# Second expert layer of a fused attention and mixture-of-experts kernel: fp32 second products become three fp32r products of halves, and first weights are loaded straight into two alternating places

## The chip, the cores and the metric

The kernel runs as one program on one core of a Trainium2 chip. The metric is the device time of one launch in microseconds (us); lower is better. Five engines run side by side, each with its own instruction stream in program order: PE (TensorE, matrix products; its weight loads are listed as PEld), DVE (VectorE), ACT (ScalarE), POOL (GpSimd, which also issues the indirect transfers) and SP (SyncE, which issues the plain transfers).

## The reference, cut to what matters

Attention over 4 batches, 12 heads, 448 positions, then two layers of experts over the 1,792 resulting rows. Only the second layer is touched:

```
N, D, E, F = (1792, 768, 8, 1024)
cap = N // E
...
# greedy assignment: best (token, expert) logit first, at most cap tokens an expert
...
for e in range(E):
    mask = assigned == e
    h = np.maximum(x[mask] @ w1[e], 0.0)
    out[mask] = h @ w2[e]
```

Each expert gets exactly 224 tokens. All data is fp32.

## The kernel before, in words

The second layer is `moe2`. It handles the eight experts in the order in which the assignment fills them. Per expert there are 48 *first products* (line L2063: 8 blocks f of 128 hidden columns, 6 slices k of 128 inputs; 224 tokens move against a 128x128 block of w1), a relu per block f (L2067, ACT), and 32 *second products* (L2077: two halves h of 112 tokens, two column halves of 384, 8 slices k). All operands are fp32. Four *turns* (L2051) transpose the tokens that were fetched for the next expert.

While the experts run, an `Assigner` works out which expert comes next and which tokens it has. A first round of it runs ahead of the experts, six more and a short last step run while they do. Such a round goes through all engines: `bids` (L1588 to L1611, with transposes L1598 on PE and copies L1600 on ACT), `count` (a column of comparisons each in L1678, L1680, L1682 on DVE, products L1643 on PE, transposes L1717), `settle` (L1721 to L1782, product L1752) and `put` (L1814 to L1838, products L1831). Its products stand in the same PE stream as the expert products, and PE takes its stream in order.

The place of each assigner step in the streams is fixed when the program is written, by `Pace`: a model with one clock per engine. Every piece of expert work calls `work(engine, cost, ready)`, which first writes out those assigner steps that the model would start earlier. The costs are constants in us, such as 0.19 for a first and 0.325 for a second product.

Weights come by `pump` (SP queue) in slices of 128 rows into six raw places, first the 6 slices of w1, then the 8 of w2; `split` copies each slice into `w1t` or `w2t`, odd slices on POOL (L2031), even ones on ACT (L2034). Products read the copies. The fourth w1 slice of an expert (`LATE`) waits for the fetch of its tokens, by a one-element POOL write (L2017) behind the two gathers (L2043).

Of the kernel before, what the change touches and what calls it, by code (L numbers as in the profile page):

```python
# [1933 lines left out]
def moe2(tc, consts, wt, qkv, x0, asn, w1, w2, y, out):  # L1934
# [8 lines left out]
    with ExitStack() as ctx:  # L1943
        ctx.enter_context(tc.manual_schedule())
        p2 = ctx.enter_context(tc.tile_pool(name="m2p", bufs=1, reuse_waits="tile"))
        ps = ctx.enter_context(tc.tile_pool(name="m2ps", bufs=1, space=PSUM))
        w1t, w2t = wt
        bank = [ps.tile([128, 512], F32, name=f"bank{i}") for i in range(8)]
        pg2, po3, px0 = bank[2:4], bank[4:7], bank[7]
        turns = cycle(bank[:2])  # L1950
        asn.bank, asn.counts = lambda: next(turns), lambda: next(turns)

        raws = [t[:, FF * i : FF * i + FF] for t in qkv for i in range(3)]
        xt = p2.tile([128, KD, CAP], F32, name="xtt")
        ht = p2.tile([128, KF, CAP], F32, name="ht")
        zr = x0[0]
        xgs = [p2.tile([CP, YW], F32, name=f"xg{i}") for i in range(2)]

# [3 lines left out]
        def first_product(f):  # L1962

            return (po3 + pg2)[f // 2][:, CAP * (f % 2) : CAP * (f % 2) + CAP]
# [30 lines left out]
        clock, work = pace.clock, pace.work  # L1995


        nload, nsplit = 0, 0

        arrival, there, done = {}, {}, {}  # L2000
        fetched = []
# [5 lines left out]
        def pump(eng=nc.sync, most=6):  # L2007
            nonlocal nload
            while nload < nsplit + most:
                n, first, k = piece(nload)  # L2010
                if n >= len(regs):
                    break
                if (n, first, k) == (n, True, LATE) and n:

                    if (n, 1) not in fetched:
                        break
                    nc.gpsimd.memset(raws[nload % 6][0:1, 0:1], 0.0)  # L2017
                r, w, wd = raws[nload % 6], w1 if first else w2, FF if first else DM
                clock["d"] = max(clock["d"], clock["p"] + DELAY, choice[n]) + wd * 1.43e-3
                arrival[nload] = clock["d"]  # L2020
                eng.dma_start(out=r[:, :wd], in_=w[bass.ds(regs[n], 1), 128 * k : 128 * (k + 1), :].rearrange("a p f -> p (a f)"))
                nload += 1

        def split(n, first, k):
            nonlocal nsplit
            assert piece(nsplit) == (n, first, k) and nload > nsplit
            r = raws[nsplit % 6]
# [8 lines left out]
            if nsplit > 1:  # L2036
                pump()

        def gather(n, h):
            clock["d"] = max(clock["d"], work("g", 1.03) + GATHER) + 0.97  # L2040
# [16 lines left out]
        def acc(n, pg, f, k, shared=False):  # L2057
            fs = slice(128 * f, 128 * f + 128)
            check = dict(skip_group_check=shared)

            t = max(there[n, True, k], there["x", 0, k // 3], there["x", 1, k // 3])
            done[f] = work("p", 0.19, t)
            nc.tensor.matmul(pg, lhsT=w1t[:, k, fs], rhs=xt[:, k, :], start=k == 0 and not (shared and f % 2), stop=k == KD - 1, **check)  # L2063
# [26 lines left out]

        for h in range(2):
            gather(0, h)
        for r in raws[FIRST:6]:
            nc.gpsimd.memset(r[0:1, 0:1], 0.0)
        few = nc.values_load(asn.regs[0:1, E : E + 1], engines=tuple(ALL), min_val=0, max_val=1)
        start = nload, nsplit, known, list(regs), dict(asn.__dict__)

        def experts(compact):
            nonlocal nload, nsplit, known
            nload, nsplit, known = start[:3]  # L2100
            regs[:] = start[3]
            choice[:] = [0.0]
            fetched.clear()
            asn.__dict__.update(start[4])
            arrival.update((i, 0.0) for i in range(FIRST))
            pace.start(phases(compact), g=2.0, d=3.5)
            ready.update({0: 4.5, 1: 5.5})
            split(0, True, 0)
# [5 lines left out]
            for g in turns:  # L2114
                for _ in g:
                    pass
            split(0, True, 1)
            for n in range(E):
                turns, gathered, turned = [], 0, 0
                splits = iter(range(KD) if n + 1 < E else ())  # L2120

                def ahead(t):

                    nonlocal gathered, turned
                    if n + 1 == E:
                        return
                    if known > n + 1 and gathered < 2:
                        gather(n + 1, gathered)
                        gathered += 1
                    elif t >= 17:  # L2130
                        if turned < 4 and gathered > turned // 2 and ready[turned // 2] <= clock["p"]:
                            if len(turns) == turned:
# [6 lines left out]
                        if t % 2 and nload > nsplit and arrival[nsplit] <= clock["p"] + EARLY:  # L2139
                            k = next(splits, None)  # L2140
                            if k is not None:
                                split(n + 1, True, k)

                for t in range(32):
                    k2 = t // 2 + 2
                    if n and t % 2 == 0 and 2 <= t <= 16:
                        relu(product(t // 2 - 1), t // 2 - 1)
                    if n == 0 and 7 <= t < 7 + KF:
                        split(0, False, t - 7)
                    if t % 2 == 0:  # L2150
                        if n == 0 and k2 < KD:
                            split(0, True, k2)
                        elif n and k2 < KF:
                            split(n, False, k2)
                    if n and t == 3:
                        store(n - 1, 1)
                    if t == 25:
                        store(n, 0)
                    ahead(t)
                    pump()  # L2160
                    if t < 16:
                        if n:
                            f, a = divmod(t, 2)
                            for k in range(3 * a, 3 * a + 3):
                                acc(n, product(f), f, k)
                        elif t < 6:

                            k, a = divmod(t, 2)
                            for f in range(4 * a, 4 * a + 4):
                                acc(n, first_product(f), f, k, True)  # L2170
                        elif t < 6 + KF:
                            f = t - 6
                            for k in range(3, KD):
                                acc(n, first_product(f), f, k, True)

                            for i in range(f - 1, f + 1) if f % 2 else ():
                                relu(first_product(i), i)
                    else:
# [11 lines left out]
                for k in splits:  # L2190
                    split(n + 1, True, k)
                split(n + 1, False, 0)
                split(n + 1, False, 1)
            store(E - 1, 1)

        with tc.If(few > 0):
# [7 lines left out]
SLACK = 0.3  # L2204
AHEAD = 0.5
DELAY = 3.2
EARLY = 0.3
GATHER = 1.7
FIRST = 1
LATE = 3  # L2210
# [64 lines left out]
```

## Time and profile before

| | |
|---|---|
| time, median of 3 runs | 1123.95 us (1121.79 to 1124.58) |
| the profiled execution: its time, its span | 1125.03 us, 1123.3 us |
| busy PE, DVE, ACT, POOL, share of the span | 95%, 52%, 41%, 22% |
| mean granted TensorE clock | 0.968 |

The span runs from the first to the last instruction; busy is the time in which an engine had an instruction under way. Products are pipelined: the time of one is longer than the distance to the next, and the distance is what a stream of them costs. An fp32 product appears in the trace as two records (768 records for 384 first products, 512 for 256 second ones).

### The profile page before, as it was taken

Reading aid. Unit: us, or ns where it says so; the run is one execution under the profiler, and the core shown is the slowest. Engines: PE = TensorE matmul, PEld = TensorE weight load, DVE = VectorE, ACT = ScalarE, POOL = GpSimd, SP = SyncE. Lnnn points to the kernel's source line nnn. Section 1 sums busy time; section 2 is a strip of 40 time slices with the busy share of each in tenths; the row PEclk is TensorE's granted clock in tenths of the full one; section 3 lists DMA queues with packets and bytes.
Section 4 is the critical chain, followed back from the end, with each engine's and each line's share of the span. In section 5 each row is a group of like instructions: output and inputs, shape, how many; then the busy total and the mean of one; then the engine's idle time right before and its main releaser. Section 6 shows DMA issues by size and latency. Waiting matters only on the chain. (4 is left out here: it accounts for less than half of the span.)

```text
span 1123.3 us, 16924 instructions
## 1 busy us (share of the span) xinstructions
PE 1072.6 (95%) x5360; PEld 672.4 (60%) x5360; DVE 589.6 (52%) x1565; ACT 462.9 (41%) x1043; POOL 249.4 (22%) x275
## 2 busy tenths in 40 slices
PE   8999999999998999999999998959999999999995
PEld 6555565555554555555555554548575676886782
DVE  5777877877965744455566762575546562000000
ACT  3677777677684222122422111642223232233320
POOL 4443333344201110000100201011213032033110
PEclk7899999999999999999999998958999999999998
DMA  6566566566357170627400101033665183485320
GB/s 153 124 146 148 128 153 153 117 155 141 86 165 268 44 282 31 253 106 268 163 21 29 58 29 49 11 118 136 207 216 195 66 274 133 142 274 174 131 107 27
DMA packets 81024, 153.99 MB, mean 137 GB/s; under 512 B 14270, under 2 KB 53438, under 8 KB 80768
## 3 DMA queue, kind: packets, MB, share of 16 engines
q1 hardware_dynamic: 75696, 129.20, 38.0%
q0 software_dynamic: 5200, 23.33, 6.8%
q8 instruction: 49, 0.80, 0.3%
q14 instruction: 79, 0.65, 0.2%
HBM read 113.84 MB, written 17.44 MB: 117 GB/s over the span
## 5 line engine op out<-in xcount | busy, mean ns | idle before, releaser
L962 DVE SCALAR_TENSOR_TENSOR sc<-yr,wg 128x768 bf16<-128x768 f32 x104 | 162.2, 1559 | 113.8 <-ACT yr L1127 100.3
L2077 PE MATMUL bank<-w2t,ht 128*112 128x384 f32 x512 | 176.5, 489 | 0.0
L881 PE MATMUL pg<-w1t,xt 128*128 128x512 f32 x360 | 163.2, 601 | 6.3 <-PEq L1169 5.2
L899 PE MATMUL po<-w2t,hx 128*128 128x384 f32 x480 | 163.2, 488 | 0.1
L2063 PE MATMUL bank<-xtt,w1t 128*128 128x224 f32 x768 | 156.6, 359 | 0.0
L205 DVE TENSOR_REDUCE nm<-sp 112x1 f32<-112x448 f32 x192 | 118.0, 619 | 57.9 <-PE sp L204 30.1
L2063 PEld LDWEIGHTS bank<-xtt,w1t 128*128 128x128 f32 x768 | 143.7, 192 | 4.7 <-issue 0.2
L211 ACT ACTIVATE e<-sp,nm 112x448 f32<-112x448 f32 x192 | 122.0, 636 | 52.9 <-DVE nm L205 34.2
L899 PEld LDWEIGHTS po<-w2t,hx 128*128 128x128 f32 x480 | 88.3, 190 | 58.7 <-issue 6.2
L2077 PEld LDWEIGHTS bank<-w2t,ht 128*112 128x112 f32 x512 | 86.4, 177 | 59.5 <-issue 0.7
L881 PEld LDWEIGHTS pg<-w1t,xt 128*128 128x128 f32 x360 | 67.1, 192 | 81.7 <-issue 76.9
L219 PE MATMUL tp<-ident,e 112*112 112x112 f32 x768 | 112.4, 270 | 0.4 <-DVE et L222 0.4
L232 PE MATMUL op<-et,qkv 112*64 112x448 f32 x384 | 98.9, 564 | 0.0
L219 PEld LDWEIGHTS tp<-ident,e 112*112 112x112 f32 x768 | 82.2, 135 | 26.3 <-issue 20.0
L225 ACT ACTIVATE et<-tp 112x448 f32<-112x448 f32 x144 | 78.8, 547 | 38.2 <-PE tp L219 36.7
L200 PE MATMUL sp<-bt,at 128*112 128x448 f32 x188 | 85.4, 454 | 1.0 <-DMA bt<-cut 1.0
L137 POOL TENSOR_TENSOR xn<-qkv,rr 112x512 f32<-112x512 f32 x47 | 48.1, 1055 | 109.7 <-DVE rr L128 109.7
L2067 ACT ACTIVATE ht<-bank 128x224 f32<-128x224 f32 x64 | 22.4, 357 | 107.5 <-PE bank L2063 107.3
L966 POOL DMA_INDIRECT y<-yr,ti x11 | 11.9, 1085 | 234.1 <-DVE sc L962 94.2
L200 PEld LDWEIGHTS sp<-bt,at 128*112 128x112 f32 x188 | 33.9, 180 | 47.8 <-issue 32.4
L2083 POOL DMA_INDIRECT out_dram<-x,ids x16 | 15.4, 965 | 210.6 <-ACT x L2082 210.6
L884 ACT ACTIVATE hr<-pg 128x512 f32<-128x512 f32 x30 | 17.9, 597 | 93.3 <-PE pg L881 92.0
(395 smaller groups left out, 1269.7 us busy)
## 6 DMA issues: line engine op xcount, KB each, us to landing
qkv<-in_moe_w_dram SPq DMA_DIRECT2D x104, 384.0 KB, 5.8
qkv<-in_moe_w_dram SPq DMA_DIRECT2D x48, 512.0 KB, 7.1
raw<-in_moe_w_dram SPq DMA_DIRECT2D x24, 512.0 KB, 5.8
bt<-cut SPq DMA_DIRECT2D x96, 112.0 KB, 2.3
at<-cut SPq DMA_DIRECT2D x96, 112.0 KB, 2.4
qkv<-in_v_dram SPq DMA_DIRECT2D x12, 448.0 KB, 6.6
xs<-xp SPq DMA_DIRECT2D x24, 224.0 KB, 2.9
qkv<-in_k_dram SPq DMA_DIRECT2D x11, 448.0 KB, 4.4
```

The source lines that it names most:

```text
L137: eng.tensor_tensor(out=xns[i][:, t].rearrange("p c h d -> p h c d"), in0=raws[i // 2][:, t, 2 * j : 2 * j + 2, :].rearrange("p h (c d) -> ...
L200: nc.tensor.matmul(sp, lhsT=at[:, h, cs], rhs=bt[:, h, :], start=h == 0, stop=h == 1)
L205: nc.vector.tensor_reduce(out=st["nm"][:, n : n + 1], in_=sp, axis=AX.X, op=OP.max, negate=True)
L211: nc.scalar.activation(e, st.pop(("s", n)), AF.Exp, bias=st["nm"][:, n : n + 1], accum_out=st["sm"][:, n : n + 1])
L219: nc.tensor.transpose(tp[:, kc, :], e[:, kc * CP : (kc + 1) * CP], ident[:CP, :CP])
L225: nc.scalar.activation(dst, tp, AF.Copy)
L232: nc.tensor.matmul(st["op"][h * D : (h + 1) * D, :], lhsT=raws[i // 2][:, 2, 2 * (i % 2) + h, kc * D : (kc + 1) * D], rhs=st["et"][:, h, k ...
L881: nc.tensor.matmul(pg, lhsT=xt[:, k, :], rhs=w1t[:, k, fs], start=k == 0, stop=k == KD - 1)
L899: nc.tensor.matmul(po[n], lhsT=hx[:, k, :], rhs=w2t[:, kk, cs], start=kk == 0, stop=kk == KF - 1)
L962: nc.vector.scalar_tensor_tensor(sc, yr[:, 0:DM], 1.0, wge[:, :, e], op0=OP.mult, op1=OP.mult, accum_out=yr[:, DM + e : DM + e + 1])
L2063: nc.tensor.matmul(pg, lhsT=w1t[:, k, fs], rhs=xt[:, k, :], start=k == 0 and not (shared and f % 2), stop=k == KD - 1, **check)
L2077: nc.tensor.matmul(po, lhsT=ht[:, k, ts], rhs=w2t[:, k, cs], start=k == 0, stop=k == KF - 1)
```

## The change

First products stay fp32, but w1 is loaded straight to where PE reads it, in two places that alternate by expert (`w1s[n % 2]`: `w1t`, and the memory of `w2t` seen as six slices). A slice of w1 for expert n may be loaded when n is at most `firsts + 1`; `firsts` is raised when the last first product of an expert has been written. w2 gets eight raw places. Each slice of it is split into a high half `w2h` (fp32r, by ACT) and a low half `w2l`, the difference (fp32r, by POOL). The relu gives `hh` (fp32r, ACT) and `hl`, the difference (fp32r, DVE, which reads the products' bank again). A second product is then hh*w2h + hh*w2l + hl*w2h, three fp32r products of the same size into the same bank. The model's costs become 0.38 for a first and 0.53 for a second product.

```diff
-        w1t, w2t = wt
+        w1s = wt[0], wt[1].rearrange("p k f -> p (k f)").rearrange("p (k f) -> p k f", f=FF)
+        w2h = p2.tile([128, KF, DM], F32R, name="w2h")
+        w2l = p2.tile([128, KF, DM], F32R, name="w2l")
...
-        raws = [t[:, FF * i : FF * i + FF] for t in qkv for i in range(3)]
+        raws = [qkv[i // 4][:, DM * (i % 4) : DM * (i % 4) + DM] for i in range(KF)]
...
-            while nload < nsplit + most:
+            while most is None or nload < most:
                 n, first, k = piece(nload)
-                if n >= len(regs):
+                if n >= len(regs) or (n > firsts + 1 if first else KF * n + k >= nsplit + KF):
                     break
+                r = w1s[n % 2][:, k, :] if first else raws[k]
...
-            h, wd = (w1t, FF) if first else (w2t, DM)
-            if k % 2:
-                there[n, first, k] = work("g", 0.1 + wd * 1.1e-3, arrival[nsplit])
-                nc.gpsimd.tensor_copy(out=h[:, k, :], in_=r[:, :wd])
-            else:
-                there[n, first, k] = work("s", 0.1 + wd * 8.3e-4, arrival[nsplit])
-                nc.scalar.activation(h[:, k, :], r[:, :wd], AF.Copy)
+            t = work("s", 0.1 + DM * 8.3e-4, arrival[n, False, k])
+            nc.scalar.activation(w2h[:, k, :], r, AF.Copy)
+            there[n, False, k] = work("g", DM * 2.5e-3, t)
+            nc.gpsimd.tensor_tensor(out=w2l[:, k, :], in0=r, in1=w2h[:, k, :].bitcast(F32), op=OP.subtract)
...
-            done[f] = work("p", 0.19, t)
-            nc.tensor.matmul(pg, lhsT=w1t[:, k, fs], rhs=xt[:, k, :], ...)
+            done[f] = work("p", 0.38, t)
+            nc.tensor.matmul(pg, lhsT=w1s[n % 2][:, k, fs], rhs=xt[:, k, :], ...)
...
-            there["h", f] = work("s", 0.38, done[f])
-            nc.scalar.activation(ht[:, f, :], pg, AF.Relu)
+            t = work("s", 0.38, done[f])
+            nc.scalar.activation(hh[:, f, :], pg, AF.Relu)
+            there["h", f] = work("v", 0.35, t)
+            nc.vector.scalar_tensor_tensor(hl[:, f, :], pg, 0.0, hh[:, f, :].bitcast(F32), op0=OP.max, op1=OP.subtract)
...
-                work("p", 0.325, max(there[n, False, k], there["h", k]))
+                work("p", 0.53, max(there[n, False, k], there["h", k]))
                 cs = slice(384 * i, 384 * i + 384)
-                nc.tensor.matmul(po, lhsT=ht[:, k, ts], rhs=w2t[:, k, cs], start=k == 0, stop=k == KF - 1)
+                nc.tensor.matmul(po, lhsT=hh[:, k, ts], rhs=w2h[:, k, cs], start=k == 0, stop=False)
+                nc.tensor.matmul(po, lhsT=hh[:, k, ts], rhs=w2l[:, k, cs], start=False, stop=False)
+                nc.tensor.matmul(po, lhsT=hl[:, k, ts], rhs=w2h[:, k, cs], start=False, stop=k == KF - 1)
```

The first place is on PE, in expert 0's second products, where the assigner's second round settles (L1717, L1752; `xg` are fetched tokens). Before:

```order
L1717 MATMUL bank_9530<-ident,pcs 128x128 x2
L2077 MATMUL bank_9533<-w2t,ht 112x384
L2051 MATMUL bank_9536<-ident,xg_9539 128x112 x3
L2077 MATMUL bank_9535<-w2t,ht 112x384
L2077 MATMUL bank_9533<-w2t,ht 112x384
L1752 LDWEIGHTS ones
L1752 MATMUL bank_9529<-ns,ones 128x8
```

Of the change:

```order
L1717 MATMUL bank_9532<-ident,pcs 128x128 x2
L2081 MATMUL bank_9536<-w2h,hh 112x384
L2082 MATMUL bank_9536<-w2l,hh 112x384
L2083 MATMUL bank_9536<-w2h,hl 112x384
L2053 MATMUL bank_9538<-ident,xg_9542 128x112 x3
L2081 MATMUL bank_9535<-w2h,hh 112x384
L2082 MATMUL bank_9535<-w2l,hh 112x384
L2083 MATMUL bank_9535<-w2h,hl 112x384
L1752 LDWEIGHTS ones
L1752 MATMUL bank_9531<-ns,ones 128x8
```

One row has become three. Between L1717 and L1752 there stood three second products and a turn, now there are two second products (six rows) and a turn. Over the whole layer the assigner's steps have moved to earlier experts: ahead of its last L1831 row there stood 192 first and 112 second products (into expert 3's second products); now there are 143 and 64 (near the end of expert 2's first products).

The second place is DVE, in expert 1's first products, at the same steps of a round (`hl` is the new low half). Before:

```order
L1814 TENSOR_TENSOR hid<-half,x3n 128x28
L1818 TENSOR_TENSOR place<-u,hid 128x224
L1826 TENSOR_SCALAR g_9194<-i_9179,k 128x112 x7
L1834 TENSOR_TENSOR table<-table,bank_9530 112x32
L1835 TENSOR_TENSOR sel<-table,full 112x32
```

Of the change:

```order
L2071 SCALAR_TENSOR_TENSOR hl<-bank_9533,hh 128x224
L1814 TENSOR_TENSOR hid<-half,x3n 128x28
L1818 TENSOR_TENSOR place<-u,hid 128x224
L1826 TENSOR_SCALAR g_9194<-i_9179,k 128x112 x7
L2071 SCALAR_TENSOR_TENSOR hl<-bank_9534,hh 128x224
L1834 TENSOR_TENSOR table<-table,bank_9532 112x32
L1835 TENSOR_TENSOR sel<-table,full 112x32
```

Eight `hl` rows per expert now stand among the assigner's rows on DVE.

The third place is POOL at the start of the experts (`y` holds the tokens' rows, `x_88` is the row buffer of a result). Before:

```order
L2031 COPY w1t<-qkv_86 128x1024
L2031 COPY w1t<-qkv_87 128x1024 x2
L2031 COPY w2t<-qkv_86 128x768
L2031 COPY w2t<-qkv_87 128x768 x2
L2031 COPY w2t<-qkv_86 128x768
L2043 DMA xg_9539<-y,ids 112x777
L2043 DMA xg_9540<-y,ids 112x777
L2017 MEMSET qkv_87 1x1
L2083 DMA out_dram<-x_88,ids 1792x768
```

Of the change:

```order
L2037 TENSOR_TENSOR w2l<-qkv_86,w2h 128x768 x4
L2045 DMA xg_9542<-y,ids 112x777
L2037 TENSOR_TENSOR w2l<-qkv_87,w2h 128x768
L2045 DMA xg_9543<-y,ids 112x777
L2023 MEMSET w2t 1x1
L2037 TENSOR_TENSOR w2l<-qkv_87,w2h 128x768 x3
L2089 DMA out_dram<-x_88,ids 1792x768
```

Seven copies per expert (three of 1024, four of 768 columns) have become eight subtractions of 768, and the first gathers now stand between subtractions.

## Rows read from the trace of the kernel before

**Rows 1.** The page: busy tenths in 40 equal slices of the span.
```profile
PE   8999999999998999999999998959999999999995
```

**Rows 2.** Windows in the second layer: busy time of each engine.
```profile
core 0: us, PE busy (x) PEld busy (x) DVE busy (x) ACT busy (x) POOL busy (x), PEclk, DMA share, GB/s
...
960.00:1000.00 40.00, 40.00 (x174) 30.53 (x173) 0.00 (x0) 12.39 (x23) 10.25 (x12) 1.00 0.57 188
...
sum 275.00, PE 272.19 PEld 197.94 DVE 96.80 ACT 86.09 POOL 66.31; mean PE 38.88 PEld 28.28 DVE 13.83 ACT 12.30 POOL 9.47
```

**Rows 3.** The page's costliest groups: expert products, weight loads of second ones, stores.
```profile
L2077 PE MATMUL bank<-w2t,ht 128*112 128x384 f32 x512 | 176.5, 489 | 0.0
L2063 PE MATMUL bank<-xtt,w1t 128*128 128x224 f32 x768 | 156.6, 359 | 0.0
...
L2077 PEld LDWEIGHTS bank<-w2t,ht 128*112 128x112 f32 x512 | 86.4, 177 | 59.5 <-issue 0.7
...
L2083 POOL DMA_INDIRECT out_dram<-x,ids x16 | 15.4, 965 | 210.6 <-ACT x L2082 210.6
```

**Rows 4.** Timeline of PE in the last expert: start, length, count of records.
```profile
1072.04 18.32 PE L2063 MATMUL bank<-xtt,w1t 128*128 128x224 f32 x96
1090.20 20.80 PE L2077 MATMUL bank<-w2t,ht 128*112 128x384 f32 x64
```

**Rows 5.** Timeline of PE, fp32r (L198) and fp32 (L2063); windows around both.
```profile
17.03 0.94 PE L198 MATMUL sp<-cut 64*112 64x448 f32 x2
...
17.03 0.57 PE L198 MATMUL sp<-cut 64*112 64x448 f32 x1
...
761.16 0.95 PE L2063 MATMUL bank<-xtt,w1t 128*128 128x224 f32 x2
...
761.53 0.95 PE L2063 MATMUL bank<-xtt,w1t 128*128 128x224 f32 x2
...
16.60:17.90 1.30, 1.30 (x4) 0.47 (x3) 0.20 (x1) 0.00 (x0) 0.75 (x1) 0.50 1.12 254
760.80:763.20 2.40, 2.40 (x8) 2.18 (x8) 2.08 (x10) 0.00 (x0) 1.04 (x1) 0.50 1.02 397
```

**Rows 6.** Timeline around one fp32r product (L200) in attention, PE and weight loads.
```profile
200.09 0.46 PE L200 MATMUL sp<-bt,at 128*112 128x448 f32 x1
200.39 0.55 PE L219 MATMUL tp<-ident,e 112*112 112x112 f32 x4
...
200.21 0.51 PEld L219 LDWEIGHTS tp<-ident,e 112*112 112x112 f32 x4
```

**Rows 7.** Timeline of all engines from 847 us; idle time before, and its releaser.
```profile
847.46 3.01 POOL L2031 COPY w1t<-qkv 128x1024 f32<-128x1024 f32 x3
847.50 3.02 DVE L1835 TENSOR_TENSOR sel<-table,full 112x32 f32<-112x32 f32 x1
...
851.15 0.65 PE L1598 MATMUL bank<-ident,bid 128*128 128x128 f32 x4 [2.27 <-DVE bid L1588]
```

**Rows 8.** Groups of DVE instructions by line, 765 to 942 us: busy us, mean ns.
```profile
L1780 DVE TENSOR_TENSOR busyn<-busyn,mx 128x8 f32<-128x8 f32 x6 | 4.5, 752 | 0.2
L1835 DVE TENSOR_TENSOR sel<-table,full 112x32 f32<-112x32 f32 x6 | 4.5, 750 | 0.2
```

**Rows 9.** Timeline of DVE, steps of the assigner.
```profile
904.15 0.19 DVE L1834 TENSOR_TENSOR table<-table,bank 112x32 f32<-112x32 f32 x1 [0.85 <-PE bank L1831]
...
925.00 0.17 DVE L1780 TENSOR_TENSOR busyn<-busyn,mx 128x8 f32<-128x8 f32 x1
...
941.94 0.19 DVE L1834 TENSOR_TENSOR table<-table,bank 112x32 f32<-112x32 f32 x1 [4.10 <-PE bank L1831]
```

**Rows 10.** Source lines: duration ns min/median/max, first and last start.
```profile
L106 POOL TENSOR_TENSOR sq<-qkv x22: 1887/1895/1901, 17.1 to 279.3; 112x1024 f32<-112x1024 f32 x22
...
L2031 POOL COPY w2t<-qkv x32: 822/829/847, 763.8 to 1077.6; 128x768 f32<-128x768 f32 x32
...
L167 DVE TENSOR_TENSOR cut<-pt,cut x24: 606/615/624, 14.7 to 323.5; 128x448 fp32r<-128x448 f32 x24
```

More of the change, by code (lines that the diff above doesn't have):

```diff
@@ L1951, in moe2 @@
         asn.bank, asn.counts = lambda: next(turns), lambda: next(turns)
-        raws = [t[:, FF * i : FF * i + FF] for t in qkv for i in range(3)]
+        raws = [qkv[i // 4][:, DM * (i % 4) : DM * (i % 4) + DM] for i in range(KF)]
         xt = p2.tile([128, KD, CAP], F32, name="xtt")
-        ht = p2.tile([128, KF, CAP], F32, name="ht")
+        hh = p2.tile([128, KF, CAP], F32R, name="hh")
+        hl = p2.tile([128, KF, CAP], F32R, name="hl")
         zr = x0[0]
@@ L1995, in moe2 @@
         clock, work = pace.clock, pace.work
-        nload, nsplit = 0, 0
+        nload, nsplit, firsts = 0, 0, 0
         arrival, there, done = {}, {}, {}
@@ L2016, in pump, with split @@
                         break
-                    nc.gpsimd.memset(raws[nload % 6][0:1, 0:1], 0.0)
-                r, w, wd = raws[nload % 6], w1 if first else w2, FF if first else DM
+                    nc.gpsimd.memset(r[0:1, 0:1], 0.0)
+                w, wd = (w1, FF) if first else (w2, DM)
                 clock["d"] = max(clock["d"], clock["p"] + DELAY, choice[n]) + wd * 1.43e-3
-                arrival[nload] = clock["d"]
-                eng.dma_start(out=r[:, :wd], in_=w[bass.ds(regs[n], 1), 128 * k : 128 * (k + 1), :].rearrange("a p f -> p (a f)"))
+                arrival[n, first, k] = clock["d"]
+                nc.sync.dma_start(out=r, in_=w[bass.ds(regs[n], 1), 128 * k : 128 * (k + 1), :].rearrange("a p f -> p (a f)"))
                 nload += 1
-        def split(n, first, k):
+        def split(n, k):
             nonlocal nsplit
-            assert piece(nsplit) == (n, first, k) and nload > nsplit
-            r = raws[nsplit % 6]
-            h, wd = (w1t, FF) if first else (w2t, DM)
-            if k % 2:
-                there[n, first, k] = work("g", 0.1 + wd * 1.1e-3, arrival[nsplit])
-                nc.gpsimd.tensor_copy(out=h[:, k, :], in_=r[:, :wd])
-            else:
-                there[n, first, k] = work("s", 0.1 + wd * 8.3e-4, arrival[nsplit])
-                nc.scalar.activation(h[:, k, :], r[:, :wd], AF.Copy)
+            assert KF * n + k == nsplit
+            r = raws[k]
+            t = work("s", 0.1 + DM * 8.3e-4, arrival[n, False, k])
+            nc.scalar.activation(w2h[:, k, :], r, AF.Copy)
+            there[n, False, k] = work("g", DM * 2.5e-3, t)
+            nc.gpsimd.tensor_tensor(out=w2l[:, k, :], in0=r, in1=w2h[:, k, :].bitcast(F32), op=OP.subtract)
             nsplit += 1
-            if nsplit > 1:
-                pump()
+            pump()
         def gather(n, h):
@@ L2059, in acc @@
             check = dict(skip_group_check=shared)
-            t = max(there[n, True, k], there["x", 0, k // 3], there["x", 1, k // 3])
-            done[f] = work("p", 0.19, t)
-            nc.tensor.matmul(pg, lhsT=w1t[:, k, fs], rhs=xt[:, k, :], start=k == 0 and not (shared and f % 2), stop=k == KD - 1, **check)
+            t = max(arrival[n, True, k], there["x", 0, k // 3], there["x", 1, k // 3])
+            done[f] = work("p", 0.38, t)
+            nc.tensor.matmul(pg, lhsT=w1s[n % 2][:, k, fs], rhs=xt[:, k, :], start=k == 0 and not (shared and f % 2), stop=k == KD - 1, **check)
         def relu(pg, f):
-            there["h", f] = work("s", 0.38, done[f])
-            nc.scalar.activation(ht[:, f, :], pg, AF.Relu)
+            t = work("s", 0.38, done[f])
+            nc.scalar.activation(hh[:, f, :], pg, AF.Relu)
+            there["h", f] = work("v", 0.35, t)
+            nc.vector.scalar_tensor_tensor(hl[:, f, :], pg, 0.0, hh[:, f, :].bitcast(F32), op0=OP.max, op1=OP.subtract)
         def gemm2(n, h, t):
@@ L2092, in moe2 @@
             gather(0, h)
-        for r in raws[FIRST:6]:
+        for r in [w1s[0][:, k, :] for k in range(FIRST, KD)] + raws:
             nc.gpsimd.memset(r[0:1, 0:1], 0.0)
@@ L2098, in experts @@
         def experts(compact):
-            nonlocal nload, nsplit, known
+            nonlocal nload, nsplit, known, firsts
             nload, nsplit, known = start[:3]
+            firsts = 0
             regs[:] = start[3]
@@ L2104, in experts @@
             asn.__dict__.update(start[4])
-            arrival.update((i, 0.0) for i in range(FIRST))
+            arrival.update(((0, True, k), 0.0) for k in range(FIRST))
             pace.start(phases(compact), g=2.0, d=3.5)
             ready.update({0: 4.5, 1: 5.5})
-            split(0, True, 0)
             pump()
@@ L2138, in ahead @@
                             turned += 1
[L2139 to L2142, printed above, removed]
                 for t in range(32):
@@ L2148, in experts @@
                     if n == 0 and 7 <= t < 7 + KF:
[L2149 to L2154, printed above, removed]
+                        split(0, t - 7)
+                    if t % 2 == 0 and n and k2 < KF:
+                        split(n, k2)
                     if n and t == 3:
@@ L2177, in experts @@
                                 relu(first_product(i), i)
+                        if t == 15:
+                            firsts = n + 1
                     else:
@@ L2189, in experts @@
                     ahead(17)
[L2190 to L2193, printed above, removed]
+                split(n + 1, 0)
+                split(n + 1, 1)
             store(E - 1, 1)
@@ L2206 @@
 DELAY = 3.2
-EARLY = 0.3
 GATHER = 1.7
```

4 lines of the change are left out of this document (1 added, 3 removed).

## The prediction

> **What bounds the kernel now.** I read the page's slices first: PE is at nine tenths or more in all but five of the 40 slices, so only PE's time, or a new wait of PE, can move the end [rows 1]. Then the second layer in windows: between 765 and 1040 us PE is busy 272.2 of 275 us (the granted clock is full, 1.00, the 2.4 GHz level, in the row from 960 to 1000), while ACT and POOL are busy less than a third of the time and DVE 96.8 us, nothing of that after 960 us [rows 2]. So the stage is a stream of products, and DVE's work there (the assigner) ends two thirds through it. The groups say which products: the two lines of expert products are 333 us of PE's time [rows 3]. The timeline of the last expert gives their real distance: 64 second records in 20.80 us, the last of them 0.49 long, so (20.80 - 0.49)/63 = 0.322 us a record and 0.645 a product; 96 first records in 18.32 us, so (18.32 - 0.36)/95 = 0.189 a record and 0.378 a product [rows 3, 4]. After 1090.20 + 20.80 = 1111.0 us come 12.3 us of eviction and store, which the change leaves as they are.
>
> **First products** stay fp32 of the same size: 0.378 us each, no gain. Their copies go (three per expert on POOL and three on ACT), but PE did not wait for these in a stage where it idles under 3 us of 275 [rows 2].
>
> **Second products** are the main term. The old one is two fp32 records; the new one is three fp32r records of the same 384 columns. The rows before have no stream of fp32r products this long at full clock, so I take the column time from where both kinds run at the same lowered clock, 0.50 (the 1.2 GHz level). There two fp32r products of 448 columns end 0.94 us after the first starts, and one alone takes 0.57: distance 0.37. Two fp32 records of 224 columns start at 761.16 and 761.53: also 0.37 [rows 5]. So fp32r passes twice the columns in the same time; a record of it costs half an fp32 record. At full clock that is 0.322/2 = 0.161 us, three of them 0.485, against 0.645: 0.160 less, times 256 products = 41 us saved. Bounds: if a record can be no shorter than the weight load beside it (0.177 us, 112 columns [rows 3]) a triple is 0.53 and the gain 29 us. If the load is not hidden at all, the nearest row is the fp32r product in attention, at full clock, whose successor starts 0.30 us after it, and whose own load starts only with it [rows 6]; for 384 columns that is 0.30 less 64 columns at 0.161/384, 0.27, a triple 0.82, and the change loses 0.17 x 256 = 44 us. I take 0.485: the L198 products of rows 5 carry a load each and still keep the column distance, and the fp32 first records keep 0.189 with loads of 128 columns beside them.
>
> **Splits, relu halves, loads.** ACT copies eight slices of 768 instead of three of 1024 and four of 768: near equal, and ACT is busy 12.4 of 40 us [rows 2]. POOL subtracts eight slices. A POOL instruction with two inputs took 1.895 us for 1024 columns, so 1.42 for 768, against 0.829 for a copy [rows 10]; 8 x 1.42 = 11.4 us per expert, under an expert of 35 us, and a slice is split about every 2.3 us (six first products), well ahead of the second products that read it. In expert 0 all eight come in a burst behind its loads, with two gathers between: some 13.5 us of POOL, for halves that are wanted one by one over the following 20 us or so; cover enough, but only just. DVE's `hl` is half the width of L167 (0.615 us for 448 columns, one input in the bank): 0.3 to 0.43, I take 0.4 [rows 10]. It must be done before the bank is used again, one block (2.3 us) later: after the relu and `hl` about 1.4 us remain for whatever DVE has ahead of it in the queue. After the assigner's end nothing is ahead. Loads: the bytes are the same, 188 GB/s at 40 us an expert [rows 2], some 215 at 35. The SP queue now holds w1 of expert n + 2 behind the last first product of n, and w2 behind it, but each is wanted an expert later. I cost all of this at nothing, except what follows.
>
> **The assigner loses its slack.** This is the second term, a loss. Before, the model counted a product at about half its real distance (0.19 for 0.378, 0.325 for 0.645), so more expert work than needed stood between two assigner steps on PE, and DVE waited for PE: 4.10 us before the last table row, 0.85 in a round near it [rows 9]. Only rarely was PE the one to wait; the trace shows how: at 847.46 three POOL copies run back to back for 3.01 us, the DVE instruction L1835 beside them takes 3.02, the next bid comes late, and PE stands still for 2.27 us before L1598 [rows 7]. Over six rounds L1835 and L1780 average 0.75 us each, where an undisturbed L1780 takes 0.17 [rows 8, 9]; 12 x 0.58 = 7 us in these two lines alone, and I estimate twice that, 14 us, for all of DVE. Now the costs are true and the products shorter, so both the slack and the rounds shrink. PE's part: ahead of the last L1831 row stood 192 x 0.378 + 112 x 0.645 = 145 us of expert products; about 181 us pass (761.16 to 941.94 [rows 5, 9]), so 36 us are the assigner's products, turns, the slow clock at the start and the stall. Now 143 x 0.378 + 64 x 0.485 = 85 us stand there, with the other 34: 119 us. DVE's part: 96.8 us busy (the 14 of waiting for POOL in it), 23 `hl` x 0.4 = 9, and per round four hand-overs from PE or ACT at 0.85 [rows 9], six rounds: 20 us. Together 126 us, against 119; rounds are uneven, and a PE that is early once cannot save that for the next round, so I raise 7 to 12 us of PE stalls, against the 2.8 that PE idles now [rows 2]. Bounds: none, if `hl` and POOL fall into hand-overs; and at the top all POOL work of experts 0 to 2 in DVE's way: 22 subtractions x 1.42 and ten gathers and stores of about 0.97 us [rows 3] are 41 us instead of 14, which makes 126 into 153 and the stall 34 us or a little more.
>
> The Trainium skill (GPSIMD Engine Reference, sections 1 and 4.1) speaks against this part: GpSimd shares its SBUF interfaces with VectorE, which contends when a VectorE instruction has two SBUF inputs or runs in a 2-port mode, and two-input elementwise work is about twice as slow there. Rows 7 show such a wait at its full length, three POOL instructions long; `hl` should escape it, having one input in the bank. By that rule the sum would be the top of these bounds.
>
> **Sum.** Own time of the profiled execution 1125.0. Second products -41, stalls 12 - 2.8 = +9: 1093. That execution lies 1.1 us above the median of the runs, so 1092 against 1123.95: 2.8% less. A difference under 0.3% (3.4 us) I count as none.
>
> **The rivals.**
> *Loads bound the fp32r records* at 0.177: gain 29, and the longer triples give the assigner 64 x 0.045 = 3 us back: 1125 - 29 + 9 - 3 - 1 = 1101, up to 1108. For it: the weight-load row is longer than 0.161. Against: first records keep a distance of 0.189 with their loads of that length. Chance 0.14.
> *The assigner stays ahead*, no new stalls: 1125 - 41 - 2.8 - 1 = 1080, to 1086. For it: rounds of 17 to 20 us of PE work against the same of DVE. Chance 0.13.
> *POOL holds DVE up*, the top bound: 1125 - 41 + 34 - 3 = 1115, and 1127 if a subtraction takes the 1.9 us of the 1024-column row. For it: rows 7. Against: POOL's runs are mostly single now, since slices come 2.3 us apart. Chance 0.12.
> *Exposed loads*, the other side: each fp32r product shows its load, as in rows 6. The change turns into a loss once a record shows more than 0.645/3 - 0.161 = 0.054 us of it; at the full 0.11 the time is about 1125 + 44 - 3 = 1166. Against: rows 5. Chance 0.07.
> The forecast, with stalls of 5 to 21 us: 1085 to 1101, chance 0.52. Two in a hundred are left for a late low half in expert 0 or a load that comes late.
>
> **How the numbers follow.** 1079 to 1113 takes in the forecast, both its fast neighbour and the load-bound case, and part of the POOL case: about 0.82. Faster by over 0.3%: the first three cases and three quarters of the POOL case, 0.88. Within 0.3%: 0.03. Slower: exposed loads and the worst of POOL, 0.09.
>
> **What would show it.** In the profile after: steady experts of about 35 us instead of 40; second records at 0.161 to 0.165 distance; no DVE after expert 2's first products but `hl`; PE idle before L1598, L1643 and L1831 in the first 120 us of the layer, released by DVE, with long DVE rows beside POOL subtractions; POOL subtractions near 1.4 us. Wrong would be: record distances of 0.18 or 0.27, PE waiting on `w2l` or on `hl` where the assigner is over, or a last assigner row as late as in expert 3.

## The result and the profile after

The changed kernel takes 1130.4 us (median of 6 runs, 1127.27 to 1132.08), the kernel before 1124.26 on the same chip (1121.79 to 1124.88). The ratio is 1.0056, 95% interval 1.0039 to 1.0074: 0.6% slower, where the prediction said 2.8% faster. The time lies 17 us above the top of the range. The profiled execution took 1131.96 us with a span of 1130.2 us; it is the one read here.

The page, PE's busy tenths in 40 equal slices and the granted clock in tenths:

```profile
PE   8999999999998999999999998858879899999995
PEclk7999999999999999999999998958889999999998
```

Against [rows 1], the second layer now starts with holes: from the 28th slice on 8, 8, 7, 9, 8, where there were nines, and the clock's row has an 8 from the 28th to the 30th, before in the 28th alone. The windows of the second layer, which answer to [rows 2], have it in microseconds:

```profile
core 0: us, PE busy (x) PEld busy (x) DVE busy (x) ACT busy (x) POOL busy (x), PEclk, DMA share, GB/s
765.00:800.00 35.00, 27.75 (x156) 22.16 (x156) 28.16 (x76) 10.02 (x20) 16.23 (x11) 0.90 0.41 144
800.00:840.00 40.00, 31.82 (x192) 25.57 (x192) 31.27 (x103) 9.62 (x21) 13.59 (x11) 0.84 0.51 176
840.00:880.00 40.00, 37.26 (x235) 30.57 (x235) 31.20 (x114) 9.93 (x23) 6.97 (x4) 0.95 0.38 134
880.00:920.00 40.00, 33.99 (x190) 28.48 (x189) 32.35 (x103) 10.99 (x22) 18.14 (x12) 0.91 0.48 163
920.00:960.00 40.00, 40.00 (x231) 39.68 (x230) 3.13 (x8) 13.39 (x26) 18.57 (x13) 1.00 0.60 214
...
sum 275.00, PE 250.83 PEld 225.84 DVE 132.38 ACT 82.39 POOL 112.27; mean PE 35.83 PEld 32.26 DVE 18.91 ACT 11.77 POOL 16.04
```

PE idles 24.2 us of these 275, before 2.8, and all of it lies before 920, while DVE still runs the assigner. The clock is the second thing to see: a mean of 0.90, 0.84, 0.95 and 0.91 of two levels, 1.00 and 0.50, means some 31 us at the lower one (twice what is missing to 1, times the width). They are five stretches; the first stands from 782.7 to 789.6 (0.51 in a window of its own), and its first 1.2 us lie inside the wait of PE shown below. Three of the five begin inside a gap of PE of 1.6 us or more, one half a microsecond behind such a gap, and the last behind three gaps of 1.73, 0.72 and 0.23 us in six. A gap of 1.59 us at 853.15 is not followed by one, nor was the gap of 2.27 us in [rows 7].

From 920 on the stage is as the prediction wanted it, with one difference. The timeline of PE in the last expert, to be held against [rows 4]:

```profile
1081.12 18.32 PE L2065 MATMUL bank<-xtt,w2t 128*128 128x224 f32 x96
1099.12 0.50 PE L2081 MATMUL bank<-w2h,hh 128*112 128x384 f32 x1
1099.46 0.34 PE L2082 MATMUL bank<-w2l,hh 128*112 128x384 f32 x1
...
1115.93 0.34 PE L2083 MATMUL bank<-w2h,hl 128*112 128x384 f32 x1
```

The 96 first products take 18.32 us as before. The 96 fp32r records begin (1115.93 - 1099.12)/95 = 0.177 us apart, not 0.161: a triple costs 0.531 us, and an expert 36.1 us instead of 40.0.

PE's waits between 765 and 1040 us, by the line that waits and the one that it waits for:

```profile
PE bank L1643 <- DVE g L1682: 6.9, 6, 2.1
PE bank L1831 <- DVE g L1826: 5.3, 4, 2.2
PE bank L2065 <- DVE hl L2071: 3.3, 2, 1.7
PE bank L1643 <- DVE g L1678: 2.8, 3, 1.4
PE bank L1752 <- DVE ns L1749: 2.8, 2, 1.6
PE bank L1598 <- DVE bid L1588: 2.7, 1, 2.7
```

Everything that PE waits for is DVE's. The timeline around the longest wait shows what DVE was doing:

```profile
780.13 3.59 POOL L2037 TENSOR_TENSOR w2l<-qkv,w2h 128x768 fp32r<-128x768 f32 x2 [5.41 <-ACT w2h L2035]
...
780.60 1.41 DVE L1835 TENSOR_TENSOR sel<-table,full 112x32 f32<-112x32 f32 x1
...
782.04 0.21 DVE L1836 TENSOR_REDUCE sum<-sel 112x4 f32<-112x32 f32 x1
782.28 1.45 DVE L1838 TENSOR_TENSOR ids<-sum 112x2 int32<-112x2 f32 x1
783.66 0.21 DVE L1588 TENSOR_REDUCE bid<-mn 128x8 f32<-128x64 f32 x1
...
783.92 0.47 PE L1598 MATMUL bank<-ident,bid 128*128 128x128 f32 x1 [2.73 <-DVE bid L1588]
...
792.40 4.06 DVE L1678 TENSOR_SCALAR g<-rows,bid 128x256 bf16<-128x256 f32 x1
...
792.65 3.66 POOL L2037 TENSOR_TENSOR w2l<-qkv,w2h 128x768 fp32r<-128x768 f32 x2
```

Two POOL subtractions run back to back from 780.13 to 783.72. L1835 starts into the first and ends with it, after 1.41 us, where its rows elsewhere take 0.19; L1836, one input, passes in 0.21; L1838, two inputs, starts into the second and ends with it, after 1.45 instead of 0.16. The next bid is 2.5 us late, and PE waits 2.73 for it. At 792.40 it is one L1678 that outlasts two subtractions. I summed this over all DVE rows from 757 to 925 us: what a row runs longer than the shortest of the same line and shape, where it is over 0.15 us. That gives 21 rows and **34.6 us of long rows**, against 14 rows and 13.9 us in the kernel before. Of the 21, ten have two input tensors and eleven are TENSOR_SCALAR rows with one (and a constant or a column of one value a partition), such as L1678; none of the 44 TENSOR_REDUCE rows is long, and no `hl`, which reads a bank. The subtraction itself (least, median and greatest duration in ns), and `hl`, whose 389 ns are as priced:

```profile
L2037 POOL TENSOR_TENSOR w2l<-qkv,w2h x64: 1797/1842/2156, 772.9 to 1093.8; 128x768 fp32r<-128x768 f32 x64
```

```profile
L2071 DVE SCALAR_TENSOR_TENSOR hl<-bank,hh 128x224 fp32r<-128x224 f32 x64 | 24.9, 389 | 170.5 <-ACT hh L2069 170.5
```

### The profile page after: what moved, and what is told of

It reads as the page before. It is cut to its first block, busy times and chain, and to the rows that moved or that the text cites. A ratio compares the mean times of both kernels' runs of the same rounds, so it can differ in the third digit from the quotient of the medians.

```text
span 1130.2 us, 17625 instructions
## 1 busy us (share of the span) xinstructions
PE 1056.7 (94%) x5616; PEld 724.5 (64%) x5616; DVE 633.6 (56%) x1629; ACT 463.4 (41%) x1051; POOL 316.6 (28%) x291
## 5 line engine op out<-in xcount | busy, mean ns | idle before, releaser
L2037 POOL TENSOR_TENSOR w2l<-qkv,w2h 128x768 fp32r<-128x768 f32 x64 | 118.0, 1856 | 90.3 <-ACT w2h L2035 78.9
L2071 DVE SCALAR_TENSOR_TENSOR hl<-bank,hh 128x224 fp32r<-128x224 f32 x64 | 24.9, 389 | 170.5 <-ACT hh L2069 170.5
L2081 PE MATMUL bank<-w2h,hh 128*112 128x384 f32 x256 | 92.7, 362 | 0.0
L2083 PE MATMUL bank<-w2h,hl 128*112 128x384 f32 x256 | 87.0, 340 | 0.0
L2082 PE MATMUL bank<-w2l,hh 128*112 128x384 f32 x256 | 86.6, 338 | 0.0
L2065 PE MATMUL bank<-xtt,w1t 128*128 128x224 f32 x384 | 84.8, 377 | 1.7 <-DVE hl L2071 1.7
L200 PE MATMUL sp<-bt,at 128*112 128x448 f32 x188 | 85.2, 453 | 0.8 <-DMA bt<-cut 0.8
L2065 PE MATMUL bank<-xtt,w2t 128*128 128x224 f32 x384 | 78.4, 362 | 1.6 <-DVE hl L2071 1.6
L2065 PEld LDWEIGHTS bank<-xtt,w1t 128*128 128x128 f32 x384 | 75.6, 203 | 6.6 <-issue 2.4
```

Source lines behind the costliest of these rows:

```text
L2037: nc.gpsimd.tensor_tensor(out=w2l[:, k, :], in0=r, in1=w2h[:, k, :].bitcast(F32), op=OP.subtract)
L2065: nc.tensor.matmul(pg, lhsT=w1s[n % 2][:, k, fs], rhs=xt[:, k, :], start=k == 0 and not (shared and f % 2), stop=k == KD - 1, **check)
L2081: nc.tensor.matmul(po, lhsT=hh[:, k, ts], rhs=w2h[:, k, cs], start=k == 0, stop=False)
L2082: nc.tensor.matmul(po, lhsT=hh[:, k, ts], rhs=w2l[:, k, cs], start=False, stop=False)
L2083: nc.tensor.matmul(po, lhsT=hl[:, k, ts], rhs=w2h[:, k, cs], start=False, stop=k == KF - 1)
```

## The experiments

Theory 1: POOL's subtractions hold DVE, DVE's late steps hold PE, and PE's clock falls after the gaps. Theory 2: the true costs in the model order the assigner's steps too tightly, whatever POOL does. Times are medians, ratios those to the kernel before on the same chip; kernels 1 to 4 and 5 to 8 ran together. Experiments 1, 4 and 8 leave the model's costs, and with them the order of the assigner's steps, as the changed kernel has them; the others change a cost.

**1. POOL without the subtraction**, three fp32r products all the same.

```diff
-            nc.gpsimd.tensor_tensor(out=w2l[:, k, :], in0=r, in1=w2h[:, k, :].bitcast(F32), op=OP.subtract)
...
-                nc.tensor.matmul(po, lhsT=hh[:, k, ts], rhs=w2l[:, k, cs], start=False, stop=False)
+                nc.tensor.matmul(po, lhsT=hh[:, k, ts], rhs=w2h[:, k, cs], start=False, stop=False)
```

> The change with POOL's subtraction left out: the product hh*w2l reads w2h instead, so the low half of w2 is not in the result; all streams keep their order and PE its work. Theory 1 (POOL's two-input subtractions hold DVE's assigner steps, PE then waits, and its clock falls): long DVE rows beside POOL drop from 34 us in all to under 6, PE's idle time between 760 and 920 us from 25 to under 5, no stretch at half clock after 765; 1094 to 1104 us. Theory 2 (true costs in the model leave no expert work between assigner steps, whatever POOL does): PE still idles 15 us or more, 1115 to 1130.

Measured: 1091.83 us, ratio 0.9711 (0.9695 to 0.9727). Its windows:

```profile
800.00:840.00 40.00, 40.00 (x273) 33.66 (x272) 31.44 (x141) 14.62 (x31) 4.14 (x5) 1.00 0.73 230
...
sum 275.00, PE 274.42 PEld 254.47 DVE 101.72 ACT 96.58 POOL 26.58; mean PE 39.20 PEld 36.35 DVE 14.53 ACT 13.80 POOL 3.80
```

PE idles 0.6 us, no DVE row is long, and the clock stays at 1.00 in every window of the stage. The time is even 2 us below what theory 1 was given. The same tight order, without POOL's work, costs nothing. Theory 2 alone is out.

**2. The old, loose order**: the model's costs halved, POOL left as it is.

```diff
-            done[f] = work("p", 0.38, t)
+            done[f] = work("p", 0.19, t)
...
-                work("p", 0.53, max(there[n, False, k], there["h", k]))
+                work("p", 0.265, max(there[n, False, k], there["h", k]))
```

> The change with the model's costs halved again (0.19 and 0.265), so that the assigner's steps stand further apart on PE; the work is the same. Theory 1: DVE is held by POOL as long as in the change (25 to 35 us of long rows), but expert products cover part of it: 1100 to 1118. Theory 2: the stalls are gone with the tight order, PE idles under 5 us, 1094 to 1102.

Measured: 1120.46 us, ratio 0.997 (0.9955 to 0.9984). Both expectations miss: theory 2's by far, theory 1's by 2 us in time and 4 us in long rows. More room between the steps halves neither number: PE still idles 21.3 us in the stage, long DVE rows sum to 21.2 us up to 1040, and only the time at the lower clock drops, to some 7 us. The waits are now spread until 1034 us, as the assigner is drawn out:

```profile
PE bank L2065 <- DVE hl L2071: 6.1, 5, 2.0
PE bank L2053 <- ACT xtt L2057: 5.7, 13, 0.5
PE bank L1598 <- DVE bid L1588: 4.8, 5, 1.1
PE bank L1752 <- DVE ns L1749: 4.1, 2, 2.4
```

From 840 on they return in every expert alike, about 3 us each. How much of that is POOL and how much this order was not separated.

**3. The subtraction on DVE.**

```diff
-            there[n, False, k] = work("g", DM * 2.5e-3, t)
-            nc.gpsimd.tensor_tensor(out=w2l[:, k, :], in0=r, in1=w2h[:, k, :].bitcast(F32), op=OP.subtract)
+            there[n, False, k] = work("v", 0.95, t)
+            nc.vector.tensor_tensor(out=w2l[:, k, :], in0=r, in1=w2h[:, k, :].bitcast(F32), op=OP.subtract)
```

> The change with the subtraction on DVE (model cost 0.95) instead of POOL. Theory 1: no long DVE rows but beside gathers and stores; some 20 subtractions of about 0.9 us join DVE's own work while the assigner runs, against 34 us of waiting: 1100 to 1115, PE idle 5 to 15 us. Theory 2: DVE has more to do in an order as tight, PE idles as long as in the change or longer, 1125 to 1140.

Measured: 1092.63 us, ratio 0.9721 (0.9705 to 0.9737). It computes all that the changed kernel computes and beats the kernel before by 31 us and the changed one by 38. That is 7 us below the range that theory 1 was given, which expected PE to idle 5 to 15 us. Its rows, first the windows, then the subtraction's line:

```profile
800.00:840.00 40.00, 39.97 (x267) 35.55 (x267) 31.14 (x119) 14.96 (x33) 3.52 (x4) 1.00 0.89 330
...
sum 275.00, PE 273.42 PEld 253.37 DVE 154.66 ACT 95.14 POOL 30.19; mean PE 39.06 PEld 36.20 DVE 22.09 ACT 13.59 POOL 4.31
```

```profile
L2037 DVE TENSOR_TENSOR w2l<-qkv,w2h x64: 942/958/997, 775.6 to 1055.2; 128x768 fp32r<-128x768 f32 x64
```

DVE carries 22 us more than in the changed kernel (154.7 against 132.4), and PE waits for it 23 us less. A DVE that does the work itself, in 0.96 us a slice, is held up less than one that shares with a POOL at 1.84.

**4. What sets an fp32r record's 0.177 us**: other widths in the second products of experts 4 to 7 (the moving columns, or the tokens, which are the weight columns).

```diff
-                cs = slice(384 * i, 384 * i + 384)
+                cols, toks = WIDTHS.get((n, h), (384, CP))
+                ts = slice(h * CP, h * CP + toks)
...
+                cs = slice(256 * i, 256 * i + 512) if cols == 512 else slice(384 * i, 384 * i + cols)
```

> The change with other shapes in the second products of experts 4 to 7 (moving columns and weight columns, by half of the tokens: 256/112, 320/112; 512/112, 384/96; 384/64, 256/64; 384/32, 256/32), so that columns of the result are left out. Only record distances are read. If the weight load bounds the record (0.174 us for 112 columns): 0.174 at 256, 320 and 384 moving columns, 0.215 at 512, 0.162 at 384/96, 384/64 and 384/32, 0.11 at 256/64. If the moving columns do (0.46 ns each): 0.118, 0.148, 0.236, and 0.177 at 384 whatever the weights.

Measured in one profiled execution. Groups by shape from 930 us on, PE and then the weight loads (busy us, mean ns):

```profile
L2086 PE MATMUL bank<-w2l,hh 128*112 128x384 f32 x43 | 14.4, 336 | 0.0
...
L2086 PE MATMUL bank<-w2l,hh 128*112 128x512 f32 x16 | 6.3, 395 | 0.0
...
L2086 PE MATMUL bank<-w2l,hh 128*32 128x384 f32 x16 | 5.3, 334 | 0.0
...
L2086 PE MATMUL bank<-w2l,hh 128*112 128x256 f32 x16 | 4.5, 280 | 0.0
```

```profile
L2086 PEld LDWEIGHTS bank<-w2l,hh 128*112 128x112 f32 x90 | 15.8, 176 | 0.7
...
L2086 PEld LDWEIGHTS bank<-w2l,hh 128*32 128x32 f32 x32 | 3.5, 108 | 1.2
```

With 32 weight columns the load is 68 ns shorter and the record 2 ns. With the moving columns it goes up and down: (395 - 280)/256 = 0.45 ns a column; the distances between starts are 115, 175 and 233 ns for 256, 384 and 512 columns, 0.455 ns each. And with 256 moving columns but all 112 weight columns, records start 0.11 us apart beside loads that still take 0.17:

```profile
991.55 0.28 PE L2085 MATMUL bank<-w2h,hh 128*112 128x256 f32 x1
991.56 0.17 PEld L2086 LDWEIGHTS bank<-w2l,hh 128*112 128x112 f32 x1
991.67 0.28 PE L2086 MATMUL bank<-w2l,hh 128*112 128x256 f32 x1
```

The weight load does not bound the record; the columns do.

**5. One part alone**: w1 straight to its two places, second products still fp32 on a plain copy of w2, so no low halves and no `hl`.

```diff
-            t = work("s", 0.1 + DM * 8.3e-4, arrival[n, False, k])
+            there[n, False, k] = work("s", 0.1 + DM * 8.3e-4, arrival[n, False, k])
             nc.scalar.activation(w2h[:, k, :], r, AF.Copy)
-            there[n, False, k] = work("g", DM * 2.5e-3, t)
-            nc.gpsimd.tensor_tensor(out=w2l[:, k, :], in0=r, in1=w2h[:, k, :].bitcast(F32), op=OP.subtract)
...
-                work("p", 0.53, max(there[n, False, k], there["h", k]))
+                work("p", 0.645, max(there[n, False, k], there["h", k]))
...
```

> One part alone: w1 straight to its two places and true costs in the model (0.38, 0.645), but second products kept as single fp32 products on a plain ACT copy of w2; no low halves, no hl, no POOL copies. Theory 1 (POOL's two-input work holds DVE, DVE then holds PE): with POOL all but free there are no long DVE rows, PE loses its 2.8 us of old gaps and nothing else changes, 1119 to 1123 us; the triples' 29 us are then the whole rest of the way to the 1092.6 of the kernel that subtracts on DVE. Theory 2 (the true costs make the order too tight for the assigner): gaps before L1598 and L1643 remain although POOL is free, 1128 us or more.

Measured: 1121.5 us, ratio 0.9983 (0.9972 to 0.9993). As theory 1 had it: no long DVE row, and PE idles 0.3 us:

```profile
sum 275.00, PE 274.74 PEld 200.01 DVE 81.03 ACT 88.20 POOL 28.48; mean PE 39.25 PEld 28.57 DVE 11.58 ACT 12.60 POOL 4.07
```

So this half of the change is worth 2 us, the old stalls. From here to experiment 3 it is 28.9 us, and 256 x (0.645 - 0.531) = 29.2: the triples.

**6. A shorter POOL instruction**: a one-input copy in the subtraction's place.

```diff
-            there[n, False, k] = work("g", DM * 2.5e-3, t)
-            nc.gpsimd.tensor_tensor(out=w2l[:, k, :], in0=r, in1=w2h[:, k, :].bitcast(F32), op=OP.subtract)
+            there[n, False, k] = work("g", DM * 1.1e-3, t)
+            nc.gpsimd.tensor_copy(out=w2l[:, k, :], in_=r)
```

> As the changed kernel, but POOL writes w2l by a plain one-input copy of 768 columns (0.83 us) instead of the subtraction (1.84 us); the values of the low half are so left out. Theory 1, with hold in proportion to POOL's time: 34.6 x 0.83/1.84 = 16 us of long DVE rows and 1092 + 0.45 x 38 = 1109 us; if a shorter instruction is also met less often (square of the ratio), 7 us of long rows and 1100 us. Rival 1a, only instructions with two inputs hold DVE: no long rows but those of before's kind, 1092 to 1095. Theory 2 (tight order): POOL's time is no matter, above 1120.

Measured: 1106.88 us, ratio 0.9852 (0.9836 to 0.9867), and 15.3 us of long DVE rows from 765 us on. That is the value in proportion to POOL's time, 1109 and 16; rival 1a falls, since a copy holds DVE as well:

```profile
821.36 4.52 DVE L1826 TENSOR_SCALAR g<-i,k 128x112 bf16<-128x112 bf16 x5
...
822.71 3.12 POOL L2037 CAST w2l<-qkv 128x768 fp32r<-128x768 f32 x4
...
825.94 0.22 PE L1831 MATMUL bank<-place,g 128*112 128x32 bf16 x1 [3.46 <-DVE g L1826]
```

The last of the five L1826 took 3.86 us, from 822.02 up to the end of the fourth copy (its first 0.7 us stood beside the issue of a store, L2089), and PE waited 3.46 for it.

**7. DVE subtracts while the assigner runs (experts 0 to 4), POOL from expert 5 on.**

```diff
-            there[n, False, k] = work("g", DM * 2.5e-3, t)
-            nc.gpsimd.tensor_tensor(out=w2l[:, k, :], in0=r, in1=w2h[:, k, :].bitcast(F32), op=OP.subtract)
+            there[n, False, k] = work(*(("v", 0.95) if n < 5 else ("g", DM * 2.5e-3)), t)
+            eng = nc.vector if n < 5 else nc.gpsimd
+            eng.tensor_tensor(out=w2l[:, k, :], in0=r, in1=w2h[:, k, :].bitcast(F32), op=OP.subtract)
```

> As the changed kernel, but the subtractions of experts 0 to 4 (while the assigner runs) are done by DVE, those of experts 5 to 15 by POOL. Theory 1: POOL does harm only while the assigner's chain runs between DVE and PE, so 1091 to 1095 us, experts 5 to 15 at 36.1 us each as in both kernels. Rival: POOL's 1.84 us also holds hl or the relu's bank in the later experts, or delays w2l there, worth some 0.3 us an expert and more: 1096 us or above.

Measured: 1091.85 us, ratio 0.9718 (0.9702 to 0.9733). The same subtractions on POOL are harmless once the assigner's chain between DVE and PE is over. The sum of the stage's windows, and one place in them:

```profile
sum 275.00, PE 273.41 PEld 253.54 DVE 138.04 ACT 94.52 POOL 60.34; mean PE 39.06 PEld 36.22 DVE 19.72 ACT 13.50 POOL 8.62
...
790.74 1.22 PE L1831 MATMUL bank<-place,g 128*112 128x32 bf16 x7 [1.28 <-DVE g L1826]
...
791.40:794.80 3.40, 3.40 (x15) 3.20 (x15) 2.42 (x14) 0.00 (x0) 0.93 (x1) 0.51 0.00 0
```

Behind a lone gap of 1.28 us the clock stood at the lower level (0.51) for 3.4 us. Experiment 3 has the same gap, and its clock stayed at 1.00:

```profile
789.68 1.17 PE L1831 MATMUL bank<-place,g 128*112 128x32 bf16 x7 [1.27 <-DVE g L1826]
```

So the length of a gap does not decide by itself whether the clock falls.

**8. The subtraction in quarters.**

```diff
-            nc.gpsimd.tensor_tensor(out=w2l[:, k, :], in0=r, in1=w2h[:, k, :].bitcast(F32), op=OP.subtract)
+            for c in range(0, DM, 192):
+                cs = slice(c, c + 192)
+                nc.gpsimd.tensor_tensor(out=w2l[:, k, cs], in0=r[:, cs], in1=w2h[:, k, cs].bitcast(F32), op=OP.subtract)
```

> As the changed kernel, but each subtraction on POOL is cut into four of 192 columns (some 0.5 us each, 2 us and a little more a slice). Theory 1a, a DVE instruction waits only for the POOL instruction that is running: every hold is at most 0.5 us, long rows sum to some 10 us, 1096 to 1108 us. Theory 1b, a DVE instruction waits for the whole run of POOL instructions that stand back to back: holds stay at 1.8 us and more, long rows 35 us or above, 1128 to 1140 us.

Measured: 1122.05 us, ratio 0.999 (0.998 to 1.0). Neither expectation: of 54 long rows 50 run 0.2 to 0.5 us longer than the shortest of their kind, no more than one quarter, but two run 1.2 and 1.3 us longer and two 5.9, through nearly a whole run. Long rows sum to 31.4 us. One of the two:

```profile
833.14 6.17 DVE L1611 TENSOR_TENSOR ohb<-eq,tm 128x64 bf16<-128x64 f32 x1
833.15 6.62 POOL L2039 TENSOR_TENSOR w2l<-qkv,w2h 128x192 fp32r<-128x192 f32 x12
...
839.37 0.09 PEld L1643 LDWEIGHTS <-ohb 128*32 128x32 bf16 x1 [4.06 <-DVE ohb L1611]
```

Here one instruction of 0.22 us stands through eleven quarters. The same line took 0.58 at 783.21, inside another such run. What decides between the two was not found. The other instruction held so long is L1767 at 892.08. The two gaps of PE behind them, 5.20 and 5.37 us, are half of what it idles in the stage.

**All of them in one account.** PE's idle time is 275 less PE in each sum of windows; the time at the lower clock is worked out from the PEclk of the windows as above. The chips' medians of the kernel before lie within 0.7 us of each other.

| kernel | POOL a slice, us | long DVE rows, us | PE idle 765–1040, us | at 0.50, us | time, us |
|---|---|---|---|---|---|
| changed | 1.84 | 34.6 | 24.2 | 31 | 1130.4 |
| 8 quarters | 4 x 0.55 | 31.4 | 21.9 | 17 | 1122.05 |
| 2 loose order | 1.84 | 21.2 | 21.3 | 7 | 1120.46 |
| 6 copy | 0.83 | 15.3 | 9.8 | 6 | 1106.88 |
| 3 on DVE | 0 | 0 | 1.6 | 0 | 1092.63 |
| 7 POOL late | 0, then 1.84 | 0 | 1.6 | 3.5 | 1091.85 |
| 1 left out | 0 | 0 | 0.6 | 0 | 1091.83 |

Take experiment 3's time, add the further idle time and half of the time at the lower clock. The changed kernel comes to 1092.6 + 22.6 + 15.5 = 1130.7, the quarters to 1092.6 + 20.3 + 8.5 = 1121.4, the copy to 1092.6 + 8.2 + 3 = 1103.8, and the loose order to 1092.6 + 19.7 + 3.5 = 1115.8. But in the changed kernel PE stands idle for 5.4 of the 31 us at the lower clock, and in the quarters for 1.5 of the 17, which this counts twice; without that they come to 1128.0 and 1120.6. So the account is short everywhere, by 2, 1, 3 and 5 us. About 1 us of it lies behind the last product in the first three (13.9, 13.6 and 13.7 us from there to the end, in experiment 3 12.7); what the rest is was not found.

## Why the prediction was wrong, step by step

- **First products, loads, splits on ACT, `hl`**: as priced. 18.32 us for 96 first products, `hl` 0.389 us, no wait for `w2l` or a load among PE's waits. PE did wait for `hl`, 3.3 us in all, but only while the assigner ran, where `hl` stands behind held DVE rows. The end behind the last product, priced at 12.3 us, took 13.9 in the profiled execution; why was not found.
- **Second products, -41 us**: direction right, size off; it was -29. The step that failed is "so fp32r passes twice the columns in the same time; a record of it costs half an fp32 record", read in [rows 5] at a clock of 0.50 and carried to the full clock as half of 0.322. At full clock an fp32r column costs 0.455 ns and an fp32 one 0.322/384 = 0.84, a ratio of 1.84 and not 2. At half clock fp32r takes 0.37/448 = 0.83 ns a column, so it gains less from the faster clock than fp32 does. That is 256 x 0.046 = 12 us.
- **Loads bound the fp32r records at 0.177**: this rival had the distance to the last digit by luck, with the wrong reason; experiment 4 shows that the load is no bound.
- **Exposed loads**: did not happen.
- **The assigner loses its slack, 12 us of stalls**: this term, with the clock behind it, decided the sign. The step that failed here is DVE's loss to POOL, put at the 14 us of the kernel before; it is 34.6. With it failed the price of the POOL subtraction, 1.42 us by columns from the 1.895 us of L106 [rows 10]; it takes 1.84 (L106 multiplies a tile by itself; whether that makes it cheaper no run shows). The balance of DVE against PE was sound in what it gives: with 34.6 for 14, 126 us become 147 against 119, 28 us of stalls, where 24.2 were measured; without any loss to POOL they become 112 against 119, and experiment 1, which has this very order, idles 0.6 us. Its other terms were not measured one by one, so some of this agreement may be luck. PE idles 24.2 us instead of 12, all but 0.6 to 1.6 of it through POOL, as experiments 1, 3 and 7 show. So the tighter order, the heading of this term, costs nothing by itself.
- **What was left out: the clock.** The prediction let PE stand still at the price of the idle time alone. In [rows 7] a gap of 2.27 us had cost no more, and the kernel before shows 1.00 in every window of the stage. Here the clock fell inside gaps or shortly behind them, for 31 us in all, worth 13 to 15 (13 without the 5.4 us in which PE stood idle anyway). That the gaps bring it is argued: experiments 1 and 5, all but without gaps, keep the full clock. Which gap does is not shown, as experiments 3 and 7 differ behind the same one.
- **POOL holds DVE up**, 1115 to 1127, chance 0.12: this was the right mechanism. "Against: POOL's runs are mostly single now" was the reason to give it so little, and the trace refutes it twice: ten of the 24 subtractions up to 925 us stand back to back in twos and threes, such as those at 780.13 and 792.65, and single ones hold a row too, L1682 at 845.23 by 1.7 us. Its time was still short, by the triples and the clock, though its 34 us of stalls were more than the 24.2 measured.

The misses add up: 12 for the triples, 12 for the stalls and 13 to 15 for the clock are 37 to 39, and the time lies 38.4 us over the forecast. The rule that the prediction cited (the Trainium skill, GPSIMD Engine Reference, sections 1 and 4.1) asked for the top of the bounds, and the trace bears it out: L1835 and L1838, with two SBUF inputs, are held, L1836 with one is not, and the subtraction takes 1.84 us on POOL against 0.96 on DVE. Whether the eleven long TENSOR_SCALAR rows ran in a 2-port mode no run here shows. The Trainium skill (SBUF — State Buffer, section "SBUF: two separate sides") calls it a lock that the other engine holds for a whole instruction. The rows at 780.13 agree; experiment 8's 6.17 us behind eleven quarters are more than one instruction, and cutting the instruction up bought some 8 us.

The change is a gain of some 31 us with its subtraction on DVE, or on POOL after the assigner's end; as it stands, POOL's half of the split gives back 38.

## What to carry to other kernels

Before work goes to POOL, look at what DVE does beside it: where a chain of short DVE steps feeds PE, POOL's busy time there can come back as a loss of PE (here POOL was busy for 55 us from 765 to 920, gathers and stores included, and 38 us were lost; with instructions of 0.83 us 35 and 14), and the same work on DVE can be free. Price gaps of PE above their length, since the clock may fall behind them: here 24 us of gaps came with 31 us at the lower level. And take a record's time from rows at the clock at which it will run: a ratio of two types read at the lower clock was off by 9% at the full one.

## What was not expected of the hardware

An fp32r product costs 0.455 ns a moving column at full clock, from 256 to 512 columns, whether its weights have 32 columns or 112. Four POOL subtractions of 192 columns take 0.55 us each back to back, 2.2 us a slice, only 20% more than one of 768 (1.84). And a DVE instruction of 0.22 us can be kept waiting 6 us, through eleven of twelve POOL instructions that stand back to back, although others of its kind get in between two of them.
